# A two-branch linear attention block on one core: pk^T x as seven block products over pairs of feature groups, and W' regrouped inside SBUF

## The chip, the cores and the metric

The kernel runs on one core of one Trainium2 chip. The metric is the device time of one execution in microseconds (us), the median of the runs. Beside it there is a profile of one execution, whose span runs from the first to the last instruction. TensorE is called PE in the profile, VectorE DVE, ScalarE ACT, GpSimd POOL; SP is the engine whose queue issues most DMAs. PE's weight loads have a row of their own, PEld. SBUF is the on-chip memory, and PSUM, eight banks of 512 floats per partition, takes what PE produces.

## What is computed

The input x has 2048 tokens (S) and 640 features (D). Two branches, A and B, see the same x with weights of their own, and a gate mixes them. For one branch:

```python
q, k, v = split(x @ wqkv)                 # 32 heads of 20 features
phi = lambda t: where(t > 0, t + 1, exp(t)) + 1e-6
pq, pk = phi(q), phi(k)
kv = einsum("bhsd,bhse->bhde", pk, v)
z = einsum("bhsd->bhd", pk)
num = einsum("bhqd,bhde->bhqe", pq, kv)
den = einsum("bhqd,bhd->bhq", pq, z) + 1e-6
branch = concat_heads(num / den) @ wo
...
g = sigmoid((x * gate_w).sum(-1))
out = g * A(x) + (1 - g) * B(x)
```

The kernel does not form v. It computes G = pk^T x (640 x 640, summed over the tokens), then kv = G Wv head by head, then W' = blockdiag(kv) Wo, a 640 x 640 matrix for each branch. The output is the sum over the branches of (pq scaled by gate/den) times W'. A column of ones behind x gives z in the same product.

## The kernel before

All of it is one function, `body`, without loops on the chip. Every instruction is recorded by `op` or `dma` with its engine, an assumed cost, the buffers that it reads and writes, and a priority; `Sched.run` then puts them into an order for each engine, and `emit` writes that order with the semaphore waits. PE keeps the order in which the calls are made, while the other engines take what the assumed costs make ready first, by priority. So the order on the chip is fixed when the kernel is built, and an engine waits at the instruction that is next in it.

Features are worked on in five groups of 128: group g holds the features 5m+g, so that one DMA transpose brings G into the layout that the next product needs. Tokens come in 16 tiles of 128 (t) and four blocks of 512 (b).

The stages, in PE's order:

1. Two tiles of x are transposed on PE, and their k = x Wk computed (`k_step`, L535 and L536).
2. `k_both` (L613) computes k for both branches for the other 14 tiles: for each of five chunks of the contraction, 512 columns of A, 258 columns that hold the rest of both branches and the gate's columns, and 512 of B. From PSUM, ACT takes the exponentials (L626, L630, L667), and DVE clamps them (L640) and adds max(k, 0) (L650) to give pk in the tile PKS, features in their natural order.
3. `g_unit` computes G for one branch and one group: 16 tiles, each with a 512-column (L720) and a 129-column matmul (L721), with pk's features at a step of five as the weights. ACT copies the result (L729), DVE takes z (L732), and SP's DMA transposes it into GS. Between the tiles the queries go in through `fill`.
4. `q_unit` (L874) computes queries: 40 units of five 512-column matmuls, one for each branch, block and group; ACT takes exponential (L891) and relu (L898), DVE clamps (L901) and adds (L909). The EQ buffers hold the exponentials.
5. `t_sum` (L935) adds up pq times z over the groups on DVE; `den` sends it through a DMA transpose, a sum over four (L969), a reciprocal (L981), the gate's factor (L984), and another DMA transpose, and scales the queries (L1013).
6. `kv_unit` (L782) computes kv, which DVE masks to the heads (L762: its output has a step of five elements). `wp_burst` (L817) computes W' in two halves of the columns; ACT copies it to SBUF (L832). Its rows come in the natural order. `st` stores them to memory in five DMAs a branch, and one load brings them back grouped ("wpl").
7. `o_mm` (L1034) computes the outputs. 15 tiles' A part is computed early (`o_part`) and kept as floats (L1058), while B's kv, W' and den are made; then the B parts follow, DVE adds both (L1071), and SP stores them. The last tile is split in 512 and 128 columns (L1078, L1080).

Weights Wv and Wo of both branches are loaded at the start, behind x.

Of the kernel before, what the change touches and what calls it, by code (L numbers as in the profile page):

```python
# [11 lines left out]
D = 640  # L12
# [27 lines left out]
XS_W = 672  # L40
KB_W = 648

# [222 lines left out]
def body(nc, A_x, A_wqkv, A_wo, B_x, B_wqkv, B_wo, gate_w, out, log=None):  # L265
# [11 lines left out]
    WKW = sb("WKW", [128, 2 * NU * D], bf)  # L277
    WKC = WKW[:, 0 : NC * 2 * KB_W].rearrange("p (c x f) -> p c x f", c=NC, x=2)
    WK = {X: WKC[:, :, i, :] for i, X in enumerate(XS)}
    WQ = {X: sb("WQ" + X, [128, NC, D], bf) for X in XS}  # L280
    WV = {X: sb("WV" + X, [128, NC, D + 28], bf) for X in XS}
    WO = {X: sb("WO" + X, [128, NU, D], bf) for X in XS}
    PKS = sb("PKS", [128, 2, NT * D], bf)
    PK = {X: PKS[:, i, :] for i, X in enumerate(XS)}
    PKt = {X: PK[X].rearrange("p (t f) -> p t f", t=NT) for X in XS}
    EX = [sb("EX%d" % i, [128, NC, 512], bf) for i in range(3)]

    def slot(X, i):
        return PK[X][:, 2560 * i : 2560 * i + 2560].rearrange("p (g s) -> p g s", g=NC)

    PQ = {
        ("A", 0): EX[0],
        ("A", 1): EX[1],
        ("A", 2): EX[2],
        ("A", 3): slot("A", 0),
        ("B", 0): slot("A", 1),
        ("B", 1): slot("A", 2),
        ("B", 2): slot("A", 3),
        ("B", 3): None,
    }  # L300
    GTS = {X: WKW[:, i * NU * D : i * NU * D + NC * D].rearrange("p (g f) -> p g f", g=NC) for i, X in enumerate(XS)}
    GS = {X: sb("GS" + X, [128, NC, D], bf) for X in XS}
    KVL = {X: sb("KVL" + X, [128, NU, GR], bf) for X in XS}
    WST = {X: WKW[:, i * NU * D : (i + 1) * NU * D].rearrange("p (u f) -> p u f", u=NU) for i, X in enumerate(XS)}
    WP = {X: sb("WP" + X, [128, NC, D], bf) for X in XS}
    XNf = XN[:, :, :].rearrange("p t f -> p (t f)")
    GSf = GS["A"][:, :, :].rearrange("p c f -> p (c f)")
    PQ["B", 3] = GSf[:, 0:2560].rearrange("p (g s) -> p g s", g=NC)
    FXT = {"A": WV["A"][:, :, :].rearrange("p c f -> p (c f)")[:, 0:2048].rearrange("p (b s) -> p b s", b=NB), "B": XNf[:, 0:2048].rearrange("p (b s) -> p b s", b=NB)}
    NOA = 15  # L310
    OA = [XNf[:, 2048 + 1280 * i : 3328 + 1280 * i].bitcast(f32) for i in range(6)]
    OA += [PK["B"][:, 1280 * i : 1280 * i + 1280].bitcast(f32) for i in range(8)]
    OA += [XT[:, :, :].rearrange("p c s -> p (c s)")[:, 0:1280].bitcast(f32)]
    NEK, NEQ, NOS = 4, 4, 4
    EK = sb("EK", [128, NEK, D], bf)
    EQ = EK[:, :, :].rearrange("p k f -> p (k f)")[:, 0 : NEQ * 512].rearrange("p (k f) -> p k f", k=NEQ)
    TSB = sb("TSB", [128, NB * 1024], bf)
    OST = TSB[:, 0 : NOS * D].rearrange("p (k f) -> p k f", k=NOS)
    TSF = [TSB[:, 1024 * b : 1024 * b + 1024].bitcast(f32) for b in range(NB)]
    TSH = sb("TSH", [128, NB, 512], bf)  # L320
    ZC = sb("ZC", [128, 2 * NC], f32)
    DNT = sb("DNT", [128, NB, 128], f32)
    TTR = sb("TTR", [128, NB, 4, 128], bf)
    FF = sb("FF", [128, NB, 512], bf)
# [3 lines left out]
    GG = sb("GG", [128, 2, NT], f32)  # L328
    ONE = sb("ONE", [128, 2], bf)
    SCR = sb("SCR", [128, 1], f32)  # L330
    EPSC = sb("EPSC", [128, 1], f32)
    PS = nc.alloc_psum_tensor("ps", [128, 8, 512], f32)


    IDN = sb("IDN", [128, 128], bf)
    BDM = CST[:, 0:24]
    BDE = CST[64:104, 24:32]

    sch = Sched({"ps": 8, "ek": NEK, "eq": NEQ, "os": NOS})
    op = sch.op  # L340

# [28 lines left out]
    def dve4(n):  # L370
        return 150 + 0.27 * n
# [853 lines left out]
```

## Time and profile before

| what | value |
|---|---|
| median of the 3 runs (lowest to highest) | 187.58 us (187.44 to 187.89) |
| span of the profiled execution | 186.2 us |
| what lies around the span, against the median | 1.4 us |
| mean granted TensorE clock | 1.000 |
| stage with the k products, 10.2 to 48.2 us: busy PE, DVE, ACT | 37.8, 32.4, 24.6 us |
| stages with G and the queries, 48.2 to 137: busy PE, DVE, ACT | 88.2, 67.0, 53.2 us |
| last 49 us (outputs, and W' of B): busy PE, DVE, ACT | 46.6, 34.6, 15.1 us |
| HBM read and written | 10.87 and 4.26 MB |

The profile gives for each group of instructions the line of the kernel, the engine, the operation, what it writes and reads, the shape, the count, and then busy time, the mean of one, and the idle time of the engine just before it. Matmuls are pipelined, so their durations overlap: a 512-column matmul lasts 379 ns in the records, but the next one starts 216 ns after it. The chain of waits follows the work back from the last instruction, at each step to what released it. A timeline line begins with the start and the duration in us.

### The profile page before, as it was taken

The numbers are of one execution on the slowest core, as the hardware profiler recorded it, in microseconds if no ns is written. First come the engines' busy times: TensorE is split into PE (matmuls) and PEld (weight loads), VectorE is DVE, ScalarE is ACT, GpSimd is POOL, SyncE is SP. The second block draws the span as 40 slices with busy tenths as digits, with TensorE's granted clock in tenths as the row PEclk, the third lists the DMA queues.
The fourth block names the chain that finished last, engine by engine and source line by source line (L and its number), as shares of the span: only waits on it lengthen the run. The fifth ranks groups of instructions, "written<-read, shape, count | busy, mean of one in ns | idle before, by whom it ended". The sixth has DMA issues, their size and how long they took to land.

```text
span 186.2 us, 3116 instructions
## 1 busy us (share of the span) xinstructions
PE 182.4 (98%) x1204; PEld 105.8 (57%) x1227; DVE 137.2 (74%) x278; ACT 96.6 (52%) x181; POOL 1.1 (1%) x12
## 2 busy tenths in 40 slices
PE   9999999999999999999999999999999999999995
PEld 4555555555655556555556555555566555555553
DVE  2289888888733555487989899999899998159563
ACT  5265656666554546544675666888623784400001
POOL 2000000000000000000000000000000000000000
PEclk9999999999999999999999999999999999999999
DMA  7979999998006011010501402115515246622324
GB/s 225 268 150 144 273 364 369 353 179 159 4 0 39 0 35 35 4 35 6 114 0 39 84 10 56 32 43 168 178 39 118 58 77 175 189 74 110 138 108 141
DMA packets 36501, 21.37 MB, mean 115 GB/s; under 512 B 25694, under 2 KB 36230, under 8 KB 36486
## 3 DMA queue, kind: packets, MB, share of 16 engines
q1 hardware_dynamic: 36188, 20.97, 44.9%
q10 hardware_dynamic: 298, 0.20, 0.4%
q8 instruction: 9, 0.15, 0.3%
q14 instruction: 6, 0.05, 0.1%
HBM read 10.87 MB, written 4.26 MB: 81 GB/s over the span
## 4 chain that ended last, share of the span: by engine, by line
PE 93%; SPq 3%; DMA 2%; issue 1%; DVE 0%; DVEq 0%
PE ps L1034 23%; PE ps L874 23%; PE ps L613 20%; PE ps L720 18%; PE ps L721 5%; SPq L353 3%; DMA XT<-in_A_x_dram 2%; PE ps L782 2%; PE ps L817 1%; PE ps L535 0%; PE ps L536 0%; DVE TSB L1078 0%; DVEq L237 0%
## 5 line engine op out<-in xcount | busy, mean ns | idle before, releaser
L720 PE MATMUL ps<-XN,PKS 128*128 128x512 bf16 x154 | 45.8, 379 | 0.1
L891 ACT ACTIVATE EK<-ps 128x512 bf16<-128x512 f32 x40 | 23.9, 598 | 30.1 <-PE ps L874 27.0
L613 PE MATMUL ps<-WKW,XT 128*128 128x512 bf16 (+1 forms) x206 | 37.9, 343 | 0.2
L721 PE MATMUL ps<-XN,PKS 128*128 128x129 bf16 x160 | 35.2, 220 | 0.3
L613 PEld LDWEIGHTS ps<-WKW,XT 128*128 128x128 bf16 x210 | 20.3, 97 | 17.5
L720 PEld LDWEIGHTS ps<-XN,PKS 128*128 128x128 bf16 x160 | 18.8, 117 | 15.8
L650 DVE SCALAR_TENSOR_TENSOR PKS<-ps,EK 128x512 bf16<-128x512 f32 (+1 forms) x42 | 24.0, 599 | 1.0
L874 PE MATMUL ps<-XT,WQA 128*128 128x512 bf16 x98 | 24.2, 379 | 0.1
L874 PE MATMUL ps<-XT,WQB 128*128 128x512 bf16 x97 | 23.4, 380 | 0.2
L901 DVE TENSOR_SCALAR EK<-EK 128x512 bf16<-128x512 bf16 x40 | 11.5, 288 | 14.0 <-ACT EK L891 13.8
L721 PEld LDWEIGHTS ps<-XN,PKS 128*128 128x128 bf16 x160 | 18.8, 117 | 3.0
L1034 PE MATMUL ps<-WPA,EX 128*128 128x128 bf16 (+1 forms) x117 | 16.6, 297 | 0.3 <-issue 0.2
L1034 PE MATMUL ps<-WPB,PKS 128*128 128x512 bf16 (+1 forms) x117 | 16.3, 297 | 0.2
L874 PEld LDWEIGHTS ps<-XT,WQB 128*128 128x128 bf16 x100 | 10.9, 118 | 8.6 <-issue 0.4
L874 PEld LDWEIGHTS ps<-XT,WQA 128*128 128x128 bf16 x100 | 10.6, 117 | 8.1
L1034 PEld LDWEIGHTS ps<-WPB,PKS 128*128 128x128 bf16 x120 | 9.3, 98 | 7.2
L1034 PEld LDWEIGHTS ps<-WPA,EX 128*128 128x128 bf16 x120 | 9.1, 98 | 7.1 <-issue 0.4
L1080 ACT ACTIVATE TSB<-ps 128x512 bf16<-128x512 f32 x1 | 0.6, 597 | 21.9 <-PE ps L1034 21.9
L898 ACT ACTIVATE PKS<-ps 128x512 bf16<-128x512 f32 x20 | 11.9, 594 | 0.0
L640 DVE TENSOR_SCALAR EK<-EK 128x768 bf16<-128x768 bf16 (+1 forms) x28 | 9.0, 321 | 3.9 <-ACT EK L630 3.9
L667 ACT ACTIVATE EK<-ps 128x512 bf16<-128x512 f32 x14 | 8.4, 597 | 6.6 <-PE ps L613 6.6
L626 ACT ACTIVATE EK<-ps 128x512 bf16<-128x512 f32 x14 | 8.4, 597 | 6.4 <-PE ps L613 6.4
(80 smaller groups left out, 200.7 us busy)
## 6 DMA issues: line engine op xcount, KB each, us to landing
out_dram<-TSB SPq DMA_DIRECT2D x15, 160.0 KB, 1.8
XN<-in_A_x_dram SPq DMA_DIRECT2D x1, 2240.0 KB, 9.5
WKW<-in_A_wqkv_dram SPq DMA_DIRECT2D x5, 160.0 KB, 3.5
WKW<-in_B_wqkv_dram SPq DMA_DIRECT2D x5, 160.0 KB, 3.6
WQA<-in_A_wqkv_dram SPq DMA_DIRECT2D x1, 800.0 KB, 11.1
WQB<-in_B_wqkv_dram SPq DMA_DIRECT2D x1, 800.0 KB, 12.3
WVA<-in_A_wqkv_dram SPq DMA_DIRECT2D x1, 800.0 KB, 11.8
WVB<-in_B_wqkv_dram SPq DMA_DIRECT2D x1, 800.0 KB, 13.2
```

The source lines that it names most:

```text
L613: x = e.matmul(two() if i == 1 else bank(i), XT[:, c, 128 * t : 128 * t + 128], r, start=(c == 0), stop=(c == NC - 1))
L626: op("ACT", lambda e: e.activation(ekw(0, 512), bank(0), ACT.Exp), act_cost(512), ins=[ps[0]], outs=[ek, ea], name="ke")
L640: lambda e: e.tensor_scalar(ekw(lo, hi), ekw(lo, hi), 1.0, EPS, op0=ALU.min, op1=ALU.add),
L650: lambda e: e.scalar_tensor_tensor(dst, src(), 0.0, e1(), op0=ALU.max, op1=ALU.add),
L667: op("ACT", lambda e: e.activation(ekw(768, 1280), bank(2), ACT.Exp), act_cost(512), ins=[ps[2]], outs=[ek, eb], name="ke")
L720: e.matmul(a[:, 0:512], l, XN[:, t, 0:512], start=(t == 0), stop=(t == NT - 1))
L721: return e.matmul(a[:, 512 : D + 1], l, XN[:, t, 512 : D + 1], start=(t == 0), stop=(t == NT - 1))
L874: r = e.matmul(PS[:, ps.slot, :], WQ[X][:, c, g::5], XT[:, c, 512 * b : 512 * b + 512], start=(c == 0), stop=(c == NC - 1),)
L891: lambda e: e.activation(EQ[:, eq.slot, :], PS[:, ps.slot, :], ACT.Exp),
L898: op("ACT", lambda e: e.activation(PQ[X, b][:, g, :], PS[:, ps.slot, :], ACT.Relu), act_cost(512), ins=[ps], outs=[rq], name="qr")
L901: lambda e: e.tensor_scalar(EQ[:, eq.slot, :], EQ[:, eq.slot, :], 1.0, EPS, op0=ALU.min, op1=ALU.add),
L1034: r = e.matmul(a[:, l0 - lo : h0 - lo], PQ[X, b][:, g, 128 * (t % 4) : 128 * (t % 4) + 128], WP[X][:, g, l0:h0], start=(X == first and g = ...
```

## The change

**Seven products for eight.** The ten pairs of branch and group (A0 to A4, B0 to B4) are taken as five pairs of groups. For one pair, the rows are two groups of 128 features, the contraction is split into even and odd tiles, and the columns of x into two halves of 320. That is a product of 2 x 2 blocks, and the change computes it with seven block products (P1 to P7) instead of eight, from sums of blocks: `s_pair` makes three new matrices of pk and changes one in place, `t_all` makes four of x, all on DVE. `prod` runs one block product: eight matmuls of 320 or 321 columns. ACT copies three of them to SBUF as floats, DVE adds those to others, and ACT copies one more, so that both groups of the pair come out. The queries' blocks are put between the products.

**Where pk is grouped.** DVE's sums need each group's features side by side. So `k_both` now uses `k_step` (512 and 128 or 129 columns for each branch), and `k_post` reads PSUM with a step of five floats and writes the groups dense. The relu of A, and in six tiles of B too, moves to ACT, with a plain add on DVE after it.

**W'.** `st` copies the rows from the staging tile straight into the grouped one: eleven DMAs a branch, each 60 rows (one of 40) of 640 onto 12 partitions (8).

**What comes with it.** The tiles lie elsewhere; Wv and Wo are loaded later, once a pair's products have freed their place; `t_sum`'s first step moves to ACT; the 15 early partial outputs become four whose PSUM stays open (`o_a`), so that L1058 and L1071 go; den of A's blocks 2 and 3 comes last. The gate's factor of B's blocks 1 to 3 is made by four small instructions on ACT. One of the two copies of each half of B's W' moves to DVE.

The core of the diff:

```diff
+QFILL = ((3, 1, 1, 1), (2, 2, 1, 1), (2, 2, 1, 1), (2, 2, 1, 1), (2, 2, 1, 1))
+QTAIL = ((2, [7, 8]), (2, [9]), (3, [5, 6]), (3, [7]), (3, [8, 9]))
+RELUB = (3, 5, 7, 9, 11, 13)
+WPDVE = (("B", 0, 1), ("B", 1, 1))
...
+    PKv = PKS[:, 0:SSB].rearrange("p (g h j m) -> p g h j m", g=2 * NC, h=2, j=8)
+    SSv = PKS[:, SSB : SSB + NPU * 3072].rearrange("p (u k j m) -> p u k j m", u=NPU, k=3, j=8)
...
+        def evg(i):
+            return ev(i).rearrange("p (g m) -> p g m", g=NC)
+
+        def psg(ps):
+            return psw(ps, D).rearrange("p (m g) -> p g m", g=NC)
...
+            op("ACT", lambda e, i=i, ps=ps: e.activation(evg(i), psg(ps), ACT.Exp), act_cost(D), ins=[ps] + first, outs=[ek, b], name="ke")
...
+                op("ACT", lambda e, X=X, ps=ps: e.activation(pkt(X, t), psg(ps), ACT.Relu), act_cost(D), ins=[ps], outs=[rk], name="kr")
+                o = op(
+                    "DVE",
+                    lambda e, X=X, i=i: e.tensor_tensor(out=pkt(X, t), in0=pkt(X, t), in1=evg(i), op=ALU.add),
...
+                    lambda e, X=X, i=i, ps=ps: e.scalar_tensor_tensor(pkt(X, t), psg(ps), 0.0, evg(i), op0=ALU.max, op1=ALU.add),
...
+    def k_both(t, relu):
+        units = []
+        for X in XS:
+            ps = Buf("k", "ps", 2)
+            for c in range(NC):
+                k_step(X, t, c, ps)
+            units.append((X, ps, X in relu))
+        k_post(t, units)
...
+    def s_pair(j):
...
+        sub(sv(0), pv(1, 0), pv(1, 1), pk, [bs1], "s1")
+        sub(sv(1), pv(0, 0), sv(0), pk + [bs1[j]], [bs2], "s2")
+        sub(sv(2), pv(0, 1), sv(1), pk + [bs2[j]], [bs4], "s4")
+        sub(pv(1, 0), pv(1, 0), pv(0, 0), pk + [bs1[j]], [bs3], "s3")
...
+    def t_all(j0, j1):
...
+        tt(0, xr(0, j0, j1), xl(0, j0, j1), ALU.subtract, [])
+        tt(1, tk(0), xr(1, j0, j1), ALU.add, [0])
+        tt(2, xr(0, j0, j1), xr(1, j0, j1), ALU.add, [])
+        tt(3, xl(1, j0, j1), tk(1), ALU.subtract, [1])
...
-            def fn(e, t=t):
-                a = psw(ps, D + 1)
-                l = PKt[X][:, t, g::5]
-                e.matmul(a[:, 0:512], l, XN[:, t, 0:512], start=(t == 0), stop=(t == NT - 1))
-                return e.matmul(a[:, 512 : D + 1], l, XN[:, t, 512 : D + 1], start=(t == 0), stop=(t == NT - 1))
...
+    def prod(g, name, ps, reg, mov, w, first, ins, after=()):
...
+                for j in range(j0, j1):
+                    r = e.matmul(PS[:, ps.slot, 0:w], reg[:, j, :], mov(j, w), start=(first and j == 0), stop=(j == 7), skip_group_check=not first)
...
+    def g_unit(g, fill):
...
+        prod(g, "P1", px, ra1, xv(0, False), W, True, lambda j: xn(j, 0) + [bpk[one[0], 2 * j]])
+        s1 = save(t1, px, HC, "p1s")
+        prod(g, "P2", py, ra2, xv(1, False), HC, True, lambda j: xn(j, 1) + [bpk[one[0], 2 * j + 1]])
+        comb(ga, 0, py, t1, "c11")
+        fill(0)
+        prod(g, "P5", pz, rs1, tv(0), W, True, lambda j: [bs1[j], bt[0, j]])
+        s5 = save(t5, pz, W, "p5s")
+        prod(g, "P6", px, rs2, tv(1), W, False, lambda j: [bs2[j], bt[1, j]], after=[s1])
+        s2 = save(t2, px, W, "u2s")
+        fill(1)
+        prod(g, "P7", px, rs3, tv(2), W, False, lambda j: [bs3[j], bt[2, j]], after=[s2])
+        c22 = comb(gb, HC, px, t5, "c22")
+        zb = zsum(two, px, t5, [c22])
+        prod(g, "P3", pz, rs4, xv(1, True), W, False, lambda j: xn(j, 1) + [bs4[j]], after=[s5])
+        c12 = comb(ga, HC, pz, t2, "c12")
+        zsum(one, pz, t2, [c12])
+        fill(2)
+        prod(g, "P4", px, rb2, tv(3), HC, False, lambda j: [bpk[two[0], 2 * j + 1], bt[3, j]], after=[c22, zb])
+        op("ACT", lambda e: e.activation(GT[:, gb.slot, 0:HC], PS[:, px.slot, 0:HC], ACT.Copy), act_cost(HC), ins=[px], outs=[gb], name="c21")
...
+            if (X, half, r) in WPDVE:
+                op("DVE", lambda e, dst=dst, src=src: e.tensor_copy(dst, src()), dve1(3 * HALF), ins=[ps[r]], outs=[bwst[X, r]], prio=-1, name="wpc")
...
-            bass.AP(tensor=WPD[X].tensor, offset=WPD[X].offset + D * row, ap=[[D, rows], [240 * D, n], [1, D]]),
-            WST[X][h : h + rows, slot : slot + n, :],
...
-            last_ld[0] = dma("SP", "wpl" + X, WP[X][:, :, :], WPD[X].rearrange("(p g) n -> p g n", g=NC), 819200, ins=bwps[X], outs=bwpm[X], prio=-1)
...
+        for k in range(n):
+            p0 = (row + 240 * k) // NC
...
+                WP[X][p0 : p0 + rows // NC, :, :],
+                WST[X, r][h : h + rows, slot + k, :],
...
+    q_next(QT[0])
+    kv_unit("B")
+    q_next(QT[1])
+    wp_burst("B", 0)
+    o_a(OA[0])
+    q_next(QT[2])
+    wp_burst("B", 1)
+    for b in range(2):
+        den("B", b)
+    o_a(OA[1])
+    q_next(len(qs))
+    for b in range(2, NB):
+        ts_ready(b + 1)
+        den("B", b)
+    o_a(OA[2])
+    for t in range(NT - 1):
+        if t in early:
+            o_mm("B", t, early[t], 0, D)
+            o_post(t, early[t], 0, D, "ACT")
+        else:
+            out_unit(t)
```

## The prediction

> **What bounds the kernel now.** I read the page's busy shares and its chain of work first, to see which engine sets the end.
>
> ```profile
> PE 182.4 (98%) x1204; PEld 105.8 (57%) x1227; DVE 137.2 (74%) x278; ACT 96.6 (52%) x181; POOL 1.1 (1%) x12
> ...
> PE 93%; SPq 3%; DMA 2%; issue 1%; DVE 0%; DVEq 0%
> ```
>
> TensorE is busy 98% of the span and is 93% of the chain; outside the start and the last store nothing else stands on it. So time can only go by giving TensorE fewer columns, and comes back wherever TensorE has to wait. Next, the timeline of TensorE at the start of the pk^T x stage, for the price of a matmul: starts, not durations, because matmuls overlap.
>
> ```profile
> 48.17 0.38 PE L720 MATMUL ps<-XN,PKS 128*128 128x512 bf16 x1
> 48.38 0.22 PE L721 MATMUL ps<-XN,PKS 128*128 128x129 bf16 x1
> 48.44 0.38 PE L720 MATMUL ps<-XN,PKS 128*128 128x512 bf16 x1
> ```
>
> A 512+129 pair takes 0.271 us start to start, and five 512s take 1.08 us in the chain (0.216 each). That leaves 0.055 for 129 columns and a slope of (216-55)/383 = 0.42 ns a column, so 321 columns are estimated at 0.136 us. Then the groups by shape, for everything else I need (last columns: busy us, mean ns of one, idle before).
>
> ```profile
> L650 DVE SCALAR_TENSOR_TENSOR PKS<-ps,EK 128x512 bf16<-128x512 f32 x28 | 19.4, 691 | 1.0
> L720 PEld LDWEIGHTS ps<-XN,PKS 128*128 128x128 bf16 x160 | 18.8, 117 | 15.8
> L613 PEld LDWEIGHTS ps<-WKW,XT 128*128 128x128 bf16 x210 | 20.3, 97 | 17.5
> L909 DVE TENSOR_TENSOR PKS<-PKS,EK 128x512 bf16<-128x512 bf16 x20 | 8.5, 423 | 2.3 <-ACT EK L891 0.5 <-ACT PKS L898 0.4
> L1013 DVE TENSOR_TENSOR EX<-EX,WVA 128x1280 bf16<-128x1280 bf16 x6 | 4.7, 817 | 0.0
> L762 DVE TENSOR_TENSOR KVLA<-ps,CST 128x480 bf16<-128x480 f32 x1 | 1.5, 1499 | 0.0
> L762 DVE TENSOR_TENSOR KVLA<-ps,CST 128x120 bf16<-128x120 f32 x1 | 0.6, 592 | 0.0
> ```
>
> L909 and L1013 price a bf16 add: 423 ns for 512 elements, 817 for 1280. L720 and L613 are weight loads with a step of five elements and with none: 117 against 97 ns. L762 is the only VectorE row whose output has a step of five elements, and it costs 1499 ns where 480 elements in a row would cost some 660 by L650. Last, ScalarE in the k stage, for what it can take in a row:
>
> ```profile
> 11.25 0.70 ACT L568 ACTIVATE EK<-ps 128x640 bf16<-128x640 f32 x1
> 11.85 0.59 ACT L626 ACTIVATE EK<-ps 128x512 bf16<-128x512 f32 x1
> ```
>
> An exponential of 640 columns occupies ScalarE 0.60 us when another follows.
>
> **The products (g_unit, prod).** Removed: 160 pairs at 0.271 = 43.4 us. Added: 5 x 56 = 280 matmuls of 320 or 321 columns at 0.136 = 38.0 us. Their loads, now without a step, are 97 ns by L613 and lie under 136. All on the path: **-5.4 us**. In the k stage a tile is now ten 512+128 pairs, 10 x 0.271 = 2.71 us, against (48.17-10.19)/14 = 2.71 before: nothing. Queries, kv, W' bursts and outputs have the same matmuls as before.
>
> **Block sums (s_pair, t_all).** These are 12 subtractions of 1280 elements (0.75 us each in a run, four L1013 in 3.02 us), 8 of 640 (estimated 0.49) and 4 of 2576 (817 + 1296 x 0.51 = 1.48). Most lie in the k stage. There VectorE has 14 clamps of 1280 (0.55, estimated from L640's 282 ns for 512 and 359 for 768), 20 adds of 640 (0.41: the 0.49 less the 0.08 by which runs overlap), 8 fused adds (0.74, L579 in a run), 13 of the subtractions and one of 2576: 7.7 + 8.2 + 5.9 + 9.4 + 1.5 = 32.7 us in 38. It keeps up. After the last k tile it owes seven subtractions, c11 and three of 2576, and would finish the first of these three 8.6 us after TensorE left the k stage. TensorE gets to the product that needs it after five queries, P1, P2 and P5: 5.4 + 3.3 = 8.7 us. I put 0 there; the cover is a tenth of a us, so a VectorE that is 1 us late costs 1 us. The other two are due at 10.8 and 14.1 us and ready at 10.1 and 11.5.
>
> **Reading PSUM by groups (k_post).** The exponentials, relus and fused adds now read PSUM with a step of five floats. No row of this trace reads PSUM so. If it is free, ScalarE needs 3 x 0.60 + 0.20 = 2.0 us for a tile with one relu and 2.6 for a tile with two, 4.6 for two tiles, where TensorE takes 5.42: hidden, with 0.12 us to spare on each of the seven instructions. Nearest rows: the weight load with this step costs 20% more (117 against 97), which makes 0.72 and 5.44 us, just even; L762, which *writes* with a step, grows by (1499-592)/360 = 2.5 ns an element, which makes some 1.7 us each, 12.2 for two tiles, and +47 us in all. A gain is excluded, since the elements are the same. I take free: the load is a read like these, L762's step is in its output, and here outputs are dense. Both ends stay as a rival.
>
> [...]
>
> **W' (wp_burst, st).** Removed: five stores and one load a branch through memory. Added: eleven transfers a branch between SBUF tiles. Issue and landing rows:
>
> ```profile
> L353 SPq DMA_DIRECT2D wpsA<-WKW x5: 327/457/721, 124.7 to 126.7; - x5
> ...
> wpsB<-WKW SPq DMA_DIRECT2D x2, 225.0 KB, 3.3
> ...
> out_dram<-TSB SPq DMA_DIRECT2D x15, 160.0 KB, 1.8
> ```
>
> Branch A's are done long before they are used. While its eleven issue (5.0 us), SP holds back two transposes of pair 4; counting back from the last product, SP is free 2.3 us before it ends, so the last transpose waits for its own data only, and the query blocks (4.3 us) cover its 2.6 us.
>
> Branch B's are late, since the partial outputs that hid the old way (L1058, 15 tiles) are down to four. Count from E, the end of the last product. TensorE does four query blocks (4.3), kv (1.43), a double block (2.16), and could start the first W' burst at E+7.9. VectorE, in its fixed order from E-2.0: comb and z (0.65), three t_sum steps (2.1), two clamp-add pairs (1.3) with one t_sum step between (0.7), reduce, t_sum, reciprocal, reduce (0.68+0.69+0.95+0.68), to E+5.7; the masks L762 (2.13 for three), to E+7.8. No wait. Then *before* its copy of the burst's PSUM stand a reciprocal (0.95), the factor (0.69) and a clamp of 1024 (0.44), then the copy itself (960 columns, estimated 1.16 from 825 for 640 at L1071): some E+10.9 with the overlaps of a run. The second burst needs that PSUM, and TensorE is there at 7.9 + 0.53 (the burst, L817) + 1.36 (a half output, five pairs) = E+9.8: **+1.1**. The next query block needs a bank that an exponential of 1024 frees (1.02); it waits for an EQ buffer that VectorE's add (0.69), behind the same copy, gives back: E+12.6, where TensorE comes at 10.9 + 0.53 = E+11.4: **+1.2**. Last, the eleven stores start when VectorE has copied the second half (add, clamp, copy: E+13.0), the last issues at E+17.6 and lands 2.8 us later (between 1.8 by the output row and 4.5 by the longest landing of wpsB): E+20.4, where TensorE, after three query blocks and three half outputs (3.2 + 4.1 from E+12.6), arrives at E+19.9: **+0.5**. Bounds of the three: 0 to 1.5, 0 to 1.5, 0 to 2.2, and 3.5 if an issue takes 0.6 as at wpsB. Below nothing is excluded, since TensorE had no gap to lose.
>
> **Den and outputs.** L1071's adds and L1058's copies go, off the path. den of A2 and A3 moves behind B's; following VectorE's queue by the same rows, A3's scaled queries are ready at about E+45.6, and tile 12 asks for them at E+47: nothing, with 1.4 us of cover. Every transpose it needs passes SP behind outputs that are ready by then.
>
> **Sum.** -5.4 + 1.1 + 1.2 + 0.5 = -2.6. The profiled execution's span goes from 186.2 to 183.6; 187.58, the median of the runs, lies 1.4 above that span, and I keep the 1.4: **185.0**.
>
> **Rivals.**
> 1. *No new wait*: VectorE runs ahead in the tail. 187.6 - 5.4 = 182.2. For it: runs of VectorE overlap by 0.07 us each. Against: three chains would all have to vanish.
> 2. *W' later still*: issues at 0.6 and landings of 4.5, or a second VectorE lag at the start of the products: 182.2 + 5 = 187.2. For it: SP's issue rows reach 0.72. Against: these transfers hold 75 KB, half an output's.
> 3. *The step in PSUM reads binds the k stage* (slower). Place: ScalarE's exponentials and relus. It decides from 0.72 us an instruction; each 0.1 above costs 7 x 7 x 0.1 = 4.9 us, so from about 0.78 the gain is gone, and twice ScalarE's dense 0.83 ns an element (598 to 969 ns over 448 elements at L891 and L832), a value between the factors 1.2 and 2.4 of the two rows, makes 1.13 us and 7 x (7 x 1.13 + 0.4 - 5.42) = +20: 205. For it: L762. Against: no PSUM row.
> 4. *It does not save what it says*: loads and matmuls of 321 columns overlap worse than here, and 0.155 each eats the 5.4: 187.6 + 2.8 = 190.4. Against: 117-ns loads beside 129 columns cost nothing here.
>
> **How the numbers follow.** Forecast 0.53, rival one 0.10, two 0.16, three 0.19, four 0.02. The range 182.0 to 188.9 holds the first three cases and the mildest of three (0.80), and takes in the bounds of the waits. About 0.3% (0.56 us) is what a measurement of this kernel tells from no change: below 187.0 lie the forecast, rival one and half of two (0.71); between 187.0 and 188.1 most of its other half (0.07); above, rivals three and four and a rest of two (0.22).
>
> **What would show it.** L-lines of prod: 280 matmuls, 0.136 start to start. In k_post, exponentials of 640 at 0.70 as at L568; 1.2 or more shows rival three, with ScalarE near 100% and TensorE idle in the k stage. Three idle stretches of TensorE in the last 60 us: before the second W' burst, before a query block, before B's first output, released by VectorE, ScalarE, DMA. Wrong would be any idle of TensorE above 1 us among the products.

## The result, and the profile after

| | before | after |
|---|---|---|
| median (lowest to highest, 4 runs each) | 187.73 us (187.44 to 187.89) | 193.89 us (193.74 to 194.57) |
| ratio of after to before, 95% interval | | 1.0345 [1.0318, 1.0372] |
| span of the profiled execution | 186.2 us | 192.2 us |
| mean granted TensorE clock | 1.000 | 0.982 |

The change makes the kernel 6.2 us slower; the forecast was 185.0. In all tables, a run more than 1.5% above the fastest of its version counts in the median and not in the ratio. The page of after, its first part and its chain of work:

```profile
PE 180.3 (94%) x1234; PEld 107.1 (56%) x1257; DVE 136.1 (71%) x259; ACT 114.9 (60%) x209; POOL 1.3 (1%) x13
...
PE 89%; SPq 3%; DMA 3%; ACT 2%; issue 1%; DVE 1%; DVEq 0%
```

TensorE was 98% busy and is now 94%. On the chain it falls from 93% to 89%; ScalarE (2%) and VectorE (1%) are new there, and DMAs rise from 2% to 3%. The groups by shape (busy us, mean ns, idle before) say where it did *not* go wrong:

```profile
L640 ACT ACTIVATE EKT<-ps 128x640 bf16<-128x640 f32 x32 | 22.3, 703 | 6.3 <-PE ps L595 5.7
...
L855 PE MATMUL ps<-TX,PKS 128*128 128x321 bf16 (+1 forms) x160 | 24.7, 300 | 0.0
```

The exponentials read PSUM with a step of five floats and take 703 ns, as the dense ones of 640 did before (0.70). The products show no idle time ahead of them, and inside one the matmuls start 0.137 us apart, where 0.136 was forecast. TensorE's timeline from the last product on (start, duration; in brackets the idle time before it and what ended it):

```profile
121.47 1.26 PE L855 MATMUL ps<-TX,PKS 128*128 128x320 bf16 x8
122.57 4.48 PE L798 MATMUL ps<-XT,WQB 128*128 128x512 bf16 x20
129.82 2.10 PE L980 MATMUL ps<-GSB,PKS 128*128 128x120 bf16 x30 [2.78 <-DMA GSB<-WKW]
132.15 3.06 PE L798 MATMUL ps<-XT,WQB 128*128 128x512 bf16 x9 [0.22 <-issue]
...
138.90 3.19 PE L798 MATMUL ps<-XT,WQB 128*128 128x512 bf16 x14 [1.11 <-ACT EQ L820]
141.92 4.24 PE L1147 MATMUL ps<-PKS,PQ 128*128 128x512 bf16 x30
150.27 0.97 PE L1147 MATMUL ps<-PKS,PQ 128*128 128x512 bf16 x6 [4.11 <-DMA PKS<-TX]
```

The last product ends at 122.73. After it come three waits: 2.8 us before kv of B (L980), for the last transpose of G; 1.1 before a query block; 4.1 before the first B output, for the regrouped W'. SP's queue in the same stretch:

```profile
119.44 4.74 SPq L397 DMA_DIRECT2D PKS<-PKS  x6
124.22 1.46 SPq L397 DMA_TRANSPOSE DEN<-DEN  x1
125.73 2.60 SPq L397 DMA_TRANSPOSE GSB<-WKW  x2
128.37 8.13 SPq L397 DMA_TRANSPOSE XN<-XN  x3
139.01 8.78 SPq L397 DMA_DIRECT2D PKS<-TX  x11
```

A's last six transfers and a transpose of den hold SP until 125.7. ScalarE had the last block of G ready at 123.2, and its transpose is issued only at 127.0. B's eleven take 8.78 us to issue, from 139.0 to 147.8, and the first B output cannot start before the last of them has landed. One issue of SP, minimum, median and maximum in ns:

```profile
L397 SPq DMA_DIRECT2D PKS<-TX x11: 682/765/785, 139.0 to 147.1; - x11
```

The two long waits cost more than their length. Windows of after (the columns from the left: stretch and its length, busy us of PE, PEld, DVE, ACT, POOL, then the granted clock, the DMA engines' share and GB/s):

```profile
129.80:131.00 1.20, 1.18 (x20) 1.20 (x21) 0.44 (x2) 0.00 (x0) 0.00 (x0) 0.86 0.51 104
131.00:134.00 3.00, 2.78 (x18) 1.63 (x18) 2.96 (x5) 0.00 (x0) 0.00 (x0) 0.50 0.53 42
...
151.00:154.00 3.00, 2.80 (x12) 1.45 (x12) 2.97 (x5) 0.70 (x1) 0.00 (x0) 0.52 0.05 14
154.00:155.00 1.00, 1.00 (x7) 0.54 (x6) 1.00 (x2) 0.14 (x1) 0.00 (x0) 0.73 0.41 145
```

From at most 0.9 us behind each of the two waits, TensorE works for some 3.4 us at half its clock, which is the 0.982 of the whole run: 1.2 x 0.14 + 3.0 x 0.50 = 1.7 us lost the first time, 3.0 x 0.48 + 1.0 x 0.27 = 1.7 the second. Together 2.8 + 1.1 + 4.1 + 0.4 (small waits) + 3.4 = 11.8 us. The span grew by 6.0, so the rest of the change brought -5.8, where the forecast had -5.4 for the products. By their own starts the products gave 43.4 - 280 x 0.137 = 5.0 of it; where the other 0.8 lies was not taken apart.

### The profile page after: what moved, and what is told of

It is laid out like the page before. It is cut to its first block, busy times and chain, and to the rows that moved or that the text cites. A ratio compares the mean times of both kernels' runs of the same rounds, so it can differ in the third digit from the quotient of the medians.

```text
span 192.2 us, 3185 instructions
## 1 busy us (share of the span) xinstructions
PE 180.3 (94%) x1234; PEld 107.1 (56%) x1257; DVE 136.1 (71%) x259; ACT 114.9 (60%) x209; POOL 1.3 (1%) x13
## 4 chain that ended last, share of the span: by engine, by line
PE 89%; SPq 3%; DMA 3%; ACT 2%; issue 1%; DVE 1%; DVEq 0%
PE ps L798 21%; PE ps L1147 21%; PE ps L855 20%; PE ps L594 17%; PE ps L595 5%; SPq L397 3%; PE ps L980 2%; DMA PKS<-TX 2%; ACT EQ L820 1%; DMA GSB<-WKW 1%; PE ps L523 1%; PE ps L1011 1%; DVE TX L1025 1%; PE ps L536 1%; DVE PKS L832 0%
## 5 line engine op out<-in xcount | busy, mean ns | idle before, releaser
L594 PE MATMUL ps<-WKW,XT 128*128 128x512 bf16 x154 | 43.1, 381 | 0.0
L820 ACT ACTIVATE EQ<-ps 128x512 bf16<-128x512 f32 (+1 forms) x37 | 23.2, 631 | 20.9 <-PE ps L798 18.1
L595 PE MATMUL ps<-WKW,XT 128*128 128x128 bf16 (+1 forms) x160 | 35.2, 220 | 0.3
L1147 PE MATMUL ps<-PKS 128*128 128x512 bf16 (+1 forms) x235 | 32.5, 297 | 0.3
L1147 PEld LDWEIGHTS ps<-PKS 128*128 128x128 bf16 x240 | 18.5, 98 | 14.3
L640 ACT ACTIVATE EKT<-ps 128x640 bf16<-128x640 f32 x32 | 22.3, 703 | 6.3 <-PE ps L595 5.7
L798 PE MATMUL ps<-XT,WQB 128*128 128x512 bf16 x95 | 23.4, 391 | 1.5 <-ACT EQ L820 1.1
L855 PE MATMUL ps<-TX,PKS 128*128 128x321 bf16 (+1 forms) x160 | 24.7, 300 | 0.0
L822 ACT ACTIVATE PKS<-ps 128x512 bf16<-128x512 f32 (+1 forms) x27 | 17.3, 642 | 7.4 <-PE ps L798 7.4
L855 PE MATMUL ps<-XN,PKS 128*128 128x321 bf16 (+1 forms) x120 | 18.0, 300 | 0.0
L798 PEld LDWEIGHTS ps<-XT,WQB 128*128 128x128 bf16 x100 | 11.8, 119 | 10.3 <-issue 1.5
L1147 PE MATMUL ps<-PKS,PQ 128*128 128x512 bf16 (+1 forms) x79 | 12.8, 323 | 4.3 <-DMA PKS<-TX 4.1
L798 PEld LDWEIGHTS ps<-XT,WQA 128*128 128x128 bf16 x100 | 11.7, 117 | 8.2
L855 PEld LDWEIGHTS ps<-XN,PKS 128*128 128x128 bf16 x120 | 11.7, 98 | 5.4
```

The lines of the kernel that those rows point to most:

```text
L594: e.matmul(a[:, 0:512], l, WK[X][:, c, 0:512], start=(c == 0), stop=(c == NC - 1))
L595: return e.matmul(a[:, 512:w], l, WK[X][:, c, 512:w], start=(c == 0), stop=(c == NC - 1))
L640: op("ACT", lambda e, i=i, ps=ps: e.activation(evg(i), psg(ps), ACT.Exp), act_cost(D), ins=[ps] + first, outs=[ek, b], name="ke")
L798: r = e.matmul(PS[:, ps.slot + i, :], WQ[X][:, c, g::5], XT[:, c, 512 * b : 512 * b + 512], start=(c == 0), stop=(c == NC - 1),)
L820: op("ACT", lambda e: e.activation(ev(), pv(), ACT.Exp), act_cost(512 * n), ins=[ps], outs=[eq], name="qe")
L822: op("ACT", lambda e: e.activation(dst, pv(), ACT.Relu), act_cost(512 * n), ins=[ps], outs=[rq], after=pq_free[b], name="qr")
```

## The experiments

Two theories to begin with. **The queue**: the eleven issues of 0.77 us on SP make both the last transpose and W' late. **The chain**: kv, masks, bursts and copies of B's W' are too long for the little other work that TensorE has beside them, whatever the transfers are. That other work is called cover below. A transfer's landing is the moment, or the time from its issue, at which its data is there. The early halves are the A parts of outputs that TensorE computes before B's W' is ready (`o_a`). The copy of W' is TX<-ps, on VectorE at L1025 or L1027, and `o_mm` stands at L1147 or L1149 (L1032 in the kernel before with W' inside SBUF). Each ratio is against runs of the kernel before beside that version, whose median was 187.34 to 187.67 us.

| run | median us | ratio to before, 95% interval |
|---|---|---|
| two transfers a branch, ungrouped | 196.69 | 1.0475 [1.0432, 1.0517] |
| W' through memory | 191.06 | 1.0182 [1.0145, 1.0218] |
| G's transposes first | 191.93 | 1.0236 [1.0209, 1.0264] |
| SP's and ACT's queue | 196.02 | 1.0438 [1.0405, 1.0471] |
| 60 partitions, ten transfers a branch, ungrouped | 189.83 | one run |
| clock held | 193.58 | one run |
| kernel before, W' inside SBUF | 188.30 | 1.0029 [1.0009, 1.0049] |
| GpSimd's queue | 194.50 | 1.0368 [1.0330, 1.0406] |
| two blocks moved | 190.14 | 1.0132 [1.0087, 1.0177] |
| W' by rows | 190.88 | 1.0190 [1.0144, 1.0237] |
| by rows, two blocks moved | 189.89 | 1.0132 [1.0105, 1.0159] |
| the same, a block between the bursts | 190.56 | 1.0171 [1.0134, 1.0208] |
| new tail, two blocks | 185.74 | 0.9918 [0.9901, 0.9935] |
| new tail, four blocks | 186.52 | 0.9963 [0.9933, 0.9994] |
| new tail, five blocks | 186.00 | 0.9934 [0.9918, 0.9951] |
| new tail, four blocks, memory | 184.38 | 0.9850 [0.9836, 0.9865] |
| the same with eight products | 190.95 | 1.0209 [1.0153, 1.0265] |
| new tail, two blocks, memory | 188.00 | 1.0013 [0.9982, 1.0044] |

**Two transfers a branch.**

```diff
-        for k in range(n):
...
-                WP[X][p0 : p0 + rows // NC, :, :],
-                WST[X, r][h : h + rows, slot + k, :],
...
+        if c:
+            return
...
+            WP[X][0:124, 3:5, :] if r else WP[X][0:124, 0:3, :],
+            WST[X, r][0:124, 0 : 2 if r else 3, :],
```

> Leaves out the grouping of W': each staging tile goes to the grouped tile in one transfer as it lies (two a branch, not eleven), so the output is not the reference's. All else as in the changed kernel. Theory 1, the queue: in the changed kernel each of the eleven issues holds SP for 0.77 us, which puts B's last G transpose 3.9 us behind its data (2.8 us idle before kv) and the last of B's eleven 8.1 us behind the copy (4.1 us idle before the first B output), and each gap is followed by some 5 us at a granted clock of 0.65 to 0.70 (1.7 us each). With two issues all of that should go: 193.9 - 2.8 - 4.1 - 3.4 = 183.6, at most 1 us more for what remains of the landing. Theory 2, the chain: kv, masks, bursts and copies of B's W' are too long for four early halves, whatever the transfers; then only the part of the eleven issues after the copy goes and 188 or more is left.

It became slower, not 10 us faster. SP's queue and TensorE's timeline:

```profile
117.51 4.03 SPq L397 DMA_TRANSPOSE DEN<-DEN  x1
121.59 5.95 SPq L397 DMA_TRANSPOSE GSB<-WKW  x2
...
139.70 1.28 SPq L397 DMA_DIRECT2D PKS<-TX  x2
```

```profile
130.34 2.67 PE L980 MATMUL ps<-GSB,PKS 128*128 128x120 bf16 x30 [3.15 <-DMA GSB<-WKW]
...
152.10 8.07 PE L1147 MATMUL ps<-PKS,PQ 128*128 128x512 bf16 x37 [5.16 <-DMA PKS<-TX]
```

The two issues are over at 141.0, and the data is there at 152.1: 775 KB in 12.4 us from the first issue, where the eleven took 11.2 (139.0 to 150.2). So the queue theory fails as it stood: the move lasts 11 to 12 us with many issues or with few. Nor does the wait before kv go: A's two issues are over by 117.0, but behind them the transpose of den holds SP for 4.03 us (1.46 in after), and the last transpose of G is issued at 125.0 and lands 5.2 us later. Why two large transfers are no faster was not tried.

**W' through memory again, products kept.**

```diff
-                WP[X][p0 : p0 + rows // NC, :, :],
...
+            bass.AP(tensor=WPD[X].tensor, offset=WPD[X].offset + D * row, ap=[[D, rows], [240 * D, n], [1, D]]),
...
+            dma("SP", "wpl" + X, WP[X][:, :, :], WPD[X].rearrange("(p g) n -> p g n", g=NC), ...
```

> The seven products kept, W' of both branches through memory again (five stores and one load a branch, as in the kernel before). Theory 1, the queue: A's five stores hold SP 2.8 us and not 9, so the idle time before kv goes with its slow clock (-4.5); for B, five stores (3.0), landing 3.3, a load (0.4) and its landing 4.5 make 11.2 us after the copy, as long as the eleven issues and their landing (8.1 + 3.0), so that wait stays: about 189.4. Theory 2, the chain: the wait before kv has another cause and stays too, 193 or more.

```profile
129.33 1.59 PE L980 MATMUL ps<-GSB,PKS 128*128 128x120 bf16 x30 [1.73 <-DMA GSB<-WKW]
...
136.88 0.60 PE L1013 MATMUL ps<-PKS 64*60 64x320 bf16 x15 [1.78 <-DVE TX L1027]
...
148.05 7.28 PE L1149 MATMUL ps<-PKS,PQ 128*128 128x512 bf16 x40 [3.08 <-DMA PKS<-wpsB]
```

2.8 us better than the eleven transfers, and still some 3.5 slower than the kernel before; 189.4 was expected. kv and the first B output still wait, less than before, and the third wait is VectorE's copy of the burst (1.78), which the forecast had. The wait before kv has a cause on SP here too: A's load is issued at 123.36 and the last transpose of G behind it, at 123.85, to land after 5.3 us. The transfers are a part of the loss; the rest lies in the chain and in what stands ahead of the transposes.

**G's transposes ahead of A's second six.**

```diff
+    for X, r, o in w_ops:
+        if r:
+            o.behind = gs_last[0]
```

> Changed kernel, but the second six of A's eleven transfers are issued behind B's two last G transposes on SP. Theory 1, the queue: the last G transpose is issued when its data is there (about 123.5 in place of 127.05), the 2.8 us before kv shrink to under 0.3 and the slow clock behind them goes: -4.5, while the wait of B's first output stays at 4 to 5 us: about 189.4. Theory 2 (the transposes wait for something else, such as ACT's copy or a landing slowed by other transfers): no change, 193.9.

```profile
127.30 1.60 PE L980 MATMUL ps<-GSB,PKS 128*128 128x120 bf16 x30
...
132.47 1.52 PE L1149 MATMUL ps<-PKS,PQ 128*128 128x512 bf16 x10 [0.87 <-DMA PKS<-PKS]
135.82 0.60 PE L1011 MATMUL ps<-PKS 64*60 64x320 bf16 x15 [1.82 <-DVE TX L1025]
...
148.75 6.95 PE L1149 MATMUL ps<-PKS,PQ 128*128 128x512 bf16 x40 [4.83 <-DMA PKS<-TX]
```

The wait before kv is gone, so it came from what stood ahead of the transposes. But only 2.0 us are gained of 4.5: 0.87 waits for A's W', now late itself, and 1.82 for VectorE's copy, which kv's wait had covered.

**The transfers on two queues, and on GpSimd's.**

```diff
-WQUEUE = ("SP",)
+WQUEUE = ("SP", "ACT")
```

> Changed kernel, but the eleven transfers of each branch alternate between SP's and ACT's queue. Theory 1, the queue: SP is held half as long; the wait before kv goes (-4.5), and B's last transfer is issued some 4 us after the copy instead of 8.1, so the wait of the first B output shrinks to under 1 us and its slow clock goes (-5): 184.5; ACT is held 4.6 us by its six, which may delay exponentials and cost 1 to 2 of that: 184 to 186.5. Theory 2, the chain: the wait before B's output stays above 3 us, 189 or more. If the price of 0.77 is not the queue's own but that of the transfers' descriptors shared by all queues, both queues slow each other down and the time is 190 or more.

> Changed kernel, with all 22 transfers on GpSimd's queue, which is otherwise idle there. Theory 1, the queue: SP is free, so the wait before kv goes (-4.5). B's eleven stay one after the other: if an issue takes 0.77 us there too, the first B output waits as before or a little less, since its transfers stand behind nothing: 189; if GpSimd's issues take 1.2 us, its wait grows by 4 to 5: 193. Theory 2, the chain: the wait before kv stays.

On two queues kv and the first B output wait for no DMA any more, and an issue costs no more when both queues issue at once (0.77 us on SP, 0.78 on ACT). But ScalarE pays: its own queue holds four issues of 0.78 us ahead of a copy that the products need.

```profile
123.52 2.33 PE L855 MATMUL ps<-TX,PKS 128*128 128x321 bf16 x8 [4.38 <-ACT EKT L883]
```

On GpSimd's queue an issue takes 0.58 us and SP is free: the last transpose is issued at 123.8. It lands at 131.0. Issue to landing (median of three) of the transposes from 110 us on, first in after, then here:

```profile
GSB<-WKW SPq DMA_TRANSPOSE x3, 2.7
```

```profile
GSB<-WKW SPq DMA_TRANSPOSE x3, 7.2
```

So the queue theory needs a second half: a transpose that was issued while A's transfers were under way landed late, behind the two large ones on SP's queue (5.2 us) as beside these on GpSimd's (7.2). Nor do faster issues shorten the move by much: B's landings take 3.3 us in the median of ten and 4.2 for the last, 10.2 us from the first issue.

**Other destination.**

```diff
-                WP[X][p0 : p0 + rows // NC, :, :],
+                WP[X][d0 : d0 + rows, dg, :],
```

> Changed kernel, but ten of the eleven transfers of a branch put their 60 rows onto 60 partitions as they lie, and the eleventh is left out (so W' is not grouped, and the output is not the reference's). Same bytes and rows in each transfer, other destination. If the price of 0.77 us an issue comes from the twelve partitions of five rows each, issues fall to 0.33 to 0.46 as in the rows of the kernel before, and both long waits shrink by the ratio (kv's to 0, B's first output's to about 1). If it comes from SBUF to SBUF transfers of 60 rows as such, issues stay at 0.77 and the time at 193 or so.

An issue takes 0.78 us here too, so the twelve partitions are not its cause. The last of B's transfers is issued at 145.8 us and its data is there at 148.1, so on SP's queue the issues set their pace. The time of 189.83 is one run with 20 transfers for 22, and settles nothing; its second long wait (2.6 us) was not followed by a lower clock (1.00).

**Holding the clock.**

```diff
+    for i in range(18):
...
+            lambda e, b=early[3]: e.matmul(psw(b, 512), WVA[:, 0, 0:1].to_broadcast([128, 128]), XT[:, 0, 0:512], start=False, stop=False, ...),
```

> Changed kernel with 18 more matmuls of 512 columns in TensorE's idle time before the first B output: the weights are a column of zeros, and they add nothing to an open PSUM group. 18 x 0.216 = 3.9 us of work in 4.1 us of idle time. If the granted clock of 0.64 in the 5 us after that wait comes from the wait, it goes to 1.0 there and the time falls by 1.7 us to 192.2; if it has another cause, the time stays at 193.9; if the matmuls are simply more work, it rises by up to 3.9.

```profile
127.50:130.10 2.60, 0.05 (x2) 0.04 (x2) 1.52 (x3) 1.92 (x4) 0.00 (x0) 1.00 0.71 141
130.10:134.00 3.90, 3.69 (x39) 2.54 (x41) 3.51 (x6) 0.10 (x1) 0.00 (x0) 1.00 0.67 62
...
139.20:142.00 2.80, 2.79 (x7) 1.07 (x7) 2.77 (x6) 1.24 (x3) 0.00 (x0) 0.50 0.20 55
...
151.60:155.00 3.40, 3.40 (x26) 1.94 (x25) 3.37 (x5) 1.14 (x2) 0.00 (x0) 1.00 0.05 18
```

Behind the filled wait the clock stays at 1.00. But here it also stayed up behind the unfilled 2.6 us before kv, and fell behind two shorter waits (1.1 and 1.4 us, 139 to 142), so one slow stretch was left, the early halves ended 1.8 us later, and the 18 matmuls ran 1.4 us past the point where W' had come in after. The time does not tell; that idle time brings the clock down is supported, by which rule is not.

**W' inside SBUF in the kernel before.**

```diff
-            bass.AP(tensor=WPD[X].tensor, offset=WPD[X].offset + D * row, ap=[[D, rows], [240 * D, n], [1, D]]),
...
+                WP[X][p0 : p0 + rows // NC, :, :],
```

> Kernel before, with only W' changed: eleven transfers a branch from SBUF to SBUF in place of five stores and a load. Theory 1, the queue: with 15 partial outputs as cover, B's eleven issues (8.5 us) and landing (3.0) end about as late as the way through memory did (3.0 + 3.3 + 0.4 + 4.5 = 11.2), and A's come ahead of transposes that wait for their data anyway: 187.5, between 187 and 189. Rival: the transfers hurt by themselves (they slow other transfers or TensorE's reads of SBUF) wherever they stand: 190 or more.

```profile
PE ps L1032 <- DMA WPB<-WKW: 0.6, 1, 0.6
```

With 15 partial outputs beside it, the same eleven transfers cost 0.5 us (0.2 to 0.9), inside the expected range. Their issues take as long here (8.78 us for B's), but there is enough cover.

**Moving two query blocks behind the last product.**

```diff
-QFILL = (..., (2, 2, 1, 1))
+QFILL = (..., (1, 1, 1, 1))
+QTAIL = ((2, [5]), (2, [6]), (2, [7]), (2, [8]), (2, [9]), (3, [5]), ...)
+QT = (3, 2, 0)
```

> The kernel with B's G transposes ahead of A's second six transfers (191.9 us measured), and two query blocks of B's block 2 moved from between the last pair's products to behind them, all as blocks of 512: the last product ends 2.2 us earlier and TensorE has 2.2 us more of other work while B's W' is made. Theory 1 (the way from the last product to the grouped W' has a fixed length, and only as much work as lies beside it is hidden): the wait of B's first output, 4.8 us there, shrinks by about 2.2 and the time to 189.7; if the wait gets short enough for the clock not to fall, to 188. Rival (ScalarE and VectorE are what makes W' late, and moved queries make them later): 191 to 193.

1.8 us faster, within 0.5 of what theory 1 gave. In the profiled run the first B output still waits 2.75 us, the burst 1.81 for VectorE's copy, and the clock falls once (0.991 over the run). In two of the four runs the clock stayed at 1.000, and these are the two fastest (188.8 and 189.8 us).

**W' by rows, alone and with the moved blocks.**

```diff
+    def wp_burst(X, r):
...
+            for half in range(2):
+                            if (t % 2 if t < 10 else 1) != r:
+                                continue
...
+WPAT = ((3, 2), (3, 3))
+WPDVE = ()
```

> Changed kernel with W' made in two halves of the rows, not of the columns: the first burst computes all 640 columns of the rows of one staging tile, so that its five transfers can be issued while the other burst is computed and copied. Both copies of B's bursts on ScalarE; A's second burst between the products of the pair before, so that A's transfers are issued ahead of B's last G transposes' data; the order reckons 0.77 us an issue. Theory 1: no wait before kv (-4.5), and behind B's last copy only six issues (4.6) and the landing (2.6) remain of 8.1 and 3.0, less a copy that no longer waits for VectorE (1.1 to 1.8): the first B output waits under 1.5 us: 185 to 187. Rival (the transfers move at 100 to 110 GB/s together, whatever the issue): 800 KB take 7.5 us from the first issue, which is before the last copy here, so little changes against theory 1; the wait is 2 to 3 us, 187 to 189.

> Both: W' by rows as in the run before this one, and two query blocks moved behind the last product. Theory 1: no wait above 1 us is left between the last product and the outputs: 187.5 - 5.4 = 182.2, and up to 184 with what remains of small waits of ScalarE and VectorE. Rival (exponentials and clamps of the moved queries delay the copies): 185 to 187.

> As the run before this one, with one query block between the two bursts of W' instead of ahead of the first. Theory 1: the first burst comes 1.1 us earlier if VectorE's masks are done, and its copies do not hold the second one up: within 1 us of the run before.

The first two missed what the queue theory gave; the third came within 0.7 us of the second, as expected, but through other waits (2.35 us for VectorE's masks). In the first, kv waits for a landing again: A's transfers, now earlier, had pushed the load of B's Wo (750 KB) to just ahead of the transposes. The burst by rows itself takes longer too:

```profile
130.26 1.59 PE L980 MATMUL ps<-GSB,PKS 128*128 128x120 bf16 x30 [1.93 <-DMA GSB<-WKW]
131.70 2.33 PE L798 MATMUL ps<-XT,WQB 128*128 128x512 bf16 x10
133.97 1.00 PE L1014 MATMUL ps<-PKS 64*60 64x320 bf16 x14
```

14 matmuls take 1.00 us where the burst by columns had 15 in 0.60.

**A new tail.** B's transposes first, both copies of B's bursts on ScalarE, all four early halves behind both bursts, den of B's block 0 first on SP, and an order reckoned with the measured prices of an issue and of the masks.

```diff
+WPDVE = ()
...
+QT = (3, 2, 1)
+OA = (0, 0, 4)
...
-                dve1(w * NC * n),
+                290 + 2.52 * w * NC * n,
...
-                issue=450.0,
+                issue=770.0,
```

> Changed kernel with B's G transposes ahead of A's second six transfers, the copies of B's bursts on ScalarE, the order reckoned with 0.77 us an issue, all four early halves behind both bursts, and two query blocks moved behind the last product. Theory 1, too little cover: from the last product, kv and the bursts end at about 8.5 us, the copies 1.9 later, eleven issues and the landing 11 later: 21.4; TensorE's other work lasts 10 x 1.08 + 1.43 + 1.06 + 5.4 = 18.7: a wait of 2.7 and its slow clock, 187 to 189. Rival (ScalarE or VectorE binds): more than 189.5.

> As the run before this one, with four query blocks moved. Theory 1, too little cover: 2.2 us more of other work: the wait is 0.5 or less, the clock stays up: 182.2 plus small waits, 183 to 185.5. Rival: with 12 blocks in a row ScalarE (1.0 us a block and 6 us of copies and factors beside) needs more than TensorE's 20.9 us, or the last pair's products, now with two blocks between them, wait for copies: 187 or more.

> As the run before this one, with five blocks moved. Theory 1: as with four, within 1 us, since the cover is then long enough. Rival: slower than with four by what ScalarE falls behind.

> Four query blocks moved, copies on ScalarE, W' of both branches through memory. Theory 1, too little cover: stores, load and landings take 1 to 2 us less than the eleven transfers, so no wait of B's first output at all: 183 to 185, as with the transfers or 0.5 less. Rival: ScalarE binds, and the time is that of four blocks with the transfers, 187 or more.

All four are faster than both kernels, by 0.4 to 1.5% against the kernel before. Two blocks did better than expected, four worse by 1.0 us; five and the way through memory came as expected. With two blocks and the eleven transfers, TensorE's waits for B's part are down to

```profile
PE ps L1149 <- DMA PKS<-TX: 1.2, 1, 1.2
PE ps L1149 <- ACT PKS L822: 1.0, 1, 1.0
PE ps L1011 <- DVE PKS L960: 0.4, 1, 0.4
```

and the clock is 1.000. That is 4.4 us less than the run with the same two blocks moved and the old tail (190.14). With four blocks the wait for W' is gone, but kv waits 2.2 us for its transpose: there is less time between A's first transfers and it, and the transposes of G from 110 us on land 5.0 us after their issue (median of three). Through memory this wait shrinks too:

```profile
PE ps L1149 <- ACT PKS L822: 0.9, 1, 0.9
PE ps L980 <- DMA GSB<-WKW: 0.5, 1, 0.5
```

184.38 us is the fastest version found, 1.5% (1.35 to 1.64%) below the kernel before.

**Eight products in the fastest version, and its two-block form.**

```diff
-        prod(g, "P5", pz, rs1, tv(0), W, True, ...
-        prod(g, "P6", px, rs2, tv(1), W, False, ...
...
+        block("Q1", px, one, ra1, ra2, False)
...
+        block("Q2", py, one, ra1, ra2, True)
...
+        block("Q3", pz, two, rb1, rb2, True)
...
+        block("P4", pw, two, rb1, rb2, False)
```

> The version with four moved query blocks and W' through memory (184.4 us), but each pair of groups with its eight plain block products (64 matmuls of 320 or 321 columns in place of 56), without the sums of blocks, the copies as floats and the adds behind them. Theory: the sum's first term holds from end to end: 40 matmuls more at 0.136: 184.4 + 5.4 = 189.8, between 189 and 190.5. Rival: without VectorE's sums and ScalarE's copies other waits go, and less than 4 us of difference is left: 188 or less.

> As the version with four moved query blocks and W' through memory (184.4 us), but with two moved blocks. Theory (cover): the way through memory is some 1.7 us shorter than the eleven transfers, which had 1.2 us of wait for W' and 185.7 with two blocks; so no wait for W' is left here either: 184 to 185. Rival: the two other blocks are needed: 185.7 or more.

The seven products are worth 6.6 us from end to end (190.95 less 184.38), 0.5 beyond the expected range. Where kv begins in the version with eight products, and in the one with seven:

```profile
129.19 1.59 PE L987 MATMUL ps<-GSB,PKS 128*128 128x120 bf16 x30 [0.85 <-DMA GSB<-WKW]
```

```profile
123.16 1.59 PE L980 MATMUL ps<-GSB,PKS 128*128 128x120 bf16 x30 [0.49 <-DMA GSB<-WKW]
```

Less the wait in brackets, TensorE arrives 5.7 us earlier with seven, against 40 x 0.136 = 5.4 forecast; the rest of the 6.6 is in larger waits. The two-block form missed. Its wait for W' is nearly gone (0.3 us), as expected, but kv waits 2.2 us for the last transpose and the clock falls behind it (0.50 from 128 to 130 us); with four blocks that wait was 0.5. SP's queue, first with two blocks, then with four:

```profile
119.95 1.20 SPq L397 DMA_TRANSPOSE GSB<-WKW  x1
121.68 0.35 SPq L397 DMA_DIRECT2D PKS<-wpsA  x1
122.08 1.21 SPq L397 DMA_TRANSPOSE GSB<-WKW  x1
```

```profile
117.81 3.32 SPq L397 DMA_TRANSPOSE GSB<-WKW  x2
121.17 1.27 SPq L397 DMA_TRANSPOSE XN<-XN  x1
122.63 0.44 SPq L397 DMA_DIRECT2D PKS<-wpsA  x1
```

With two blocks, the load of A's W' (800 KB) is issued 0.4 us ahead of the last transpose, which lands after 5.2 us; with four it comes behind both, and the last transpose lands after 3.1. The first run through memory had the load ahead too, and 5.3 us. No run changed this order alone.

## Why the prediction was wrong, point by point

- **The products, -5.4: right.** Their matmuls start 0.137 us apart, which makes -5.0 (with 0.136 the sum itself is 43.4 - 38.1 = 5.3); -5.8 is left in the trace once the waits are taken out, and the run with eight products shows 5.7 behind the last product.
- **Block sums at 0, with 0.1 us of cover: right.** No idle time of TensorE or its weight loads ahead of the products is above 0.3 us.
- **PSUM reads with a step of five at 0: right** (703 ns; the fused adds 820 ns, 824 in the dense row of before). Rival three was 19% of the chances and had no part. No run shows the factor of two in its 205 us: the exponential of 640 took 703 ns with the step and 702 without it.
- **"The last transpose waits for its own data only": the first step that failed.** It rested on 11 x 0.457 us of issues for branch A. The issues take 0.765 us, 9.0 in all, so SP was not free 2.3 us before the last product but 1.5 after it, with a transpose of den still in between. It was put at 0 without a bound, and cost 2.8 us and 1.7 of half clock. Putting the transposes first removed the wait. Cheaper issues for A would not have: with two of them (1.4 us in all) kv still waited 3.2 us, on GpSimd's queue 3.6, because the landing that I counted on (2.6 us) did not hold with such transfers under way (5.2 and 7.2 there).
- **Wait 1, 1.1: measured 0, since kv's own wait and the half clock behind it gave VectorE the time.** It came back as 1.8 in both runs that put the transposes first and kept the copy on VectorE, as 1.8 through memory, where kv waited 1.7 at full clock, as 1.2 on two queues, and as 1.1 in the run whose kv wait (2.6 us) had no half clock behind it. The mechanism was right, hidden behind an earlier one.
- **Wait 2, 1.2: right**, 1.1, and for the stated reason: the exponential that TensorE waits for had itself waited for VectorE's add behind the copy.
- **Wait 3, 0.5 with bounds of 0 to 2.2, or 3.5: right mechanism, wrong size, and the second step that failed.** It measured 4.1. Counted from E, the end of the last product, the copy ended at 16.3 (13.0 forecast) and TensorE arrived at 23.4 (19.9), which nearly cancel. The term that was mis-sized is the move of B's W' from the first issue to the last landing: 4.6 + 2.8 = 7.4 in the sum, 11.2 measured, of which the last of the eleven issues began after 8.1. The issue price alone does not explain it, since the move took 12.4 with two issues and 10.2 with issues of 0.58. The row I took was a store to memory; the trace held no transfer from SBUF to SBUF, and the upper bound of 0.6 was again a store's (the 4.5 for the landing was the load's). The nearest rows of another path are no bound.
- **The clock: not in the sum at all, without a reason given.** Two long waits cost 3.4 us more. The trace of before had no idle stretch (0.3 us was TensorE's longest wait), and so no row for it.
- **Rival two (W' later still, 187.2) had the mechanism, at less than half its price.** It allowed 5 us for W'; the three waits and the clock came to 11.8. No rival on the slower side had this place: I looked for it in PSUM reads.

Of the 11.7 us between the forecast without waits (182.2) and 193.9, the way of the transfers is 2.8 (through memory 191.1), and the order of the tail with the work beside it 6.7 more (184.4); 2.2 are left in the fastest version. The parts do not simply add: with two blocks in the new tail the way through memory was 2.3 us slower than the transfers (188.0 against 185.7). How the 6.7 divide among the copies on ScalarE, the early halves behind the bursts, SP's order and the moved blocks was not taken apart. The two blocks alone gave 1.8 (from 191.9 to 190.1).

## What to carry to other kernels

Where a change takes away work that hid a long chain (here eleven of fifteen early outputs), add up that chain from its first to its last link against what is left beside it, before pricing the links one by one. An operation that the trace does not show is not bounded by the same instruction on another path: measure it alone, and ask of the queue that issues it who stands behind. Look also at what stands just ahead of a small transfer that the chain waits for: here a transpose behind a large one took twice as long to land (5.2 us against 2.6). A long wait of TensorE should be given a second price, the half clock behind it: here it came behind 14 of the 21 waits of 1.9 to 5.2 us that are counted below, and cost 1.7 us both times in after.

## What the runs showed of the hardware

- Rows of 1280 bytes between SBUF tiles: an issue of 60 rows takes 0.77 us on SP's queue, 0.78 on ACT's, 0.58 on GpSimd's, and on SP's queue the same onto 12 partitions (0.765) as onto 60 (0.779). Issued alone on SP's queue (141 to 149 us in after), they moved at 86 to 101 GB/s while the DMA engines were 0.31 to 0.37 busy; the whole of W' took 10.2 to 12.4 us from the first issue, against 9.5 to 10.1 through memory.
- The granted clock fell to 0.50 behind 7 of 8 waits of 3.1 to 5.2 us, behind 7 of 13 of those of 1.9 to 2.8 (the run with five blocks left out), and behind none of 1.0 to 1.8 that stood alone. It stayed there for 3.4 us, and three times, around the longer waits, for about 6.8. The length of a wait alone does not tell: in the run with 60 partitions the clock fell behind 2.0 us and not behind 2.6. By which rule it falls was not shown.
- Bursts of small matmuls that alternate between two row groups (partitions 0 to 63 and 64 to 127 of their inputs) took 0.60 us for 15; with the same row group throughout (W' by rows), 1.00 for 14.
